# A gated linear-attention layer and a mixture of experts on one core: batches interleaved, decays scanned over 128-token blocks

## Chip, core and metric

The kernel runs on one core of a Trainium2 chip. The metric is the time of one execution in device microseconds (us), the median of the runs. The core has a matrix engine (PE, with its weight loads as PEld), a vector engine (DVE), a scalar engine (ACT), a general engine (POOL), and a sync engine (SP) that in this kernel issues DMAs only. Each engine works through its own list in order and stops at an instruction whose inputs or buffers are not ready.

## The reference

Two layers follow each other. The first is attention with a decaying state, for 4 batches, 8 heads, 768 tokens, head width 48:

```python
for t in range(S):
    state = alpha[:, :, t, :, None] * state + einsum('bhd,bhe->bhde', k[:, :, t], v[:, :, t])
    y[:, :, t] = einsum('bhd,bhde->bhe', q[:, :, t], state)
```

`alpha` lies in 0.8 to 1 and decays each key dimension by itself. The heads of a token are put side by side to x of 4 x 768 x 384. The second layer sends each token to one of 8 experts (384 to 1024 to 384 with a ReLU) and scales the result with that expert's softmax probability. The expert is the argmax of the token's logits at a batch's first token or where `local_gate < 0.5`; elsewhere it is the expert of the token before.

## The kernel before

**Blocks.** The 3072 tokens are worked in 24 blocks of 128 tokens, each of two chunks of 64, in the order of the batches: batch 0's six blocks, then batch 1's, and so on. Two heads share 112 partitions (odd head rows 0 to 47, even head rows 64 to 111), so the 8 heads are four pairs.

**One block** passes these steps (the loop is L462 to L485):

- `load`, `load_v` (L239, L250): SP issues the transfer `x` (keys, queries and decays together), two transfers into `vt` (values for the state, even and odd heads in two halves with zeros beside them) and two into `vw` (the same values again, under room for the states). These have three buffers (NP) and are asked for two blocks ahead.
- `prep` (L257): two DVE scans over 520 columns: `A`, the prefix products of the decays in each 64-token chunk (L264), and `sf`, a backward scan seeded with the reciprocal of the chunk's last product (L267). POOL multiplies keys by `sf` and queries by `A` (L268, L270).
- `kt` (L278): four PE transposes of the keys; ACT copies them out of PSUM as `kk`.
- `um` (L302): 8 matmuls give `up`, the sum of key times value for each chunk. For each chunk DVE adds it to the state (`tt`, L322) and decays the state to the chunk's end (`sn`, L323); ACT copies that state into `vw` (L327, L328). The state of one chunk is needed by the next, all through a batch.
- `pm` (L287): 16 matmuls of keys by queries into `pe`; ACT copies the scaled queries under them (L297, L298); two DVE masks of 64 partitions x 512 columns (L300) make `pq`.
- `ym` (L330): 16 matmuls, each of 112 or 128 rows, take masked products and state part in one go (L338); ACT copies the sum out as `XR` (L344).
- `xt` (L346): three transposes of x, an ACT copy `xx`, the store of x to DRAM (`xd`, L355), and three matmuls for the router's logits (L357).

**Routing** (`route`, L360) runs for every two blocks (G = 2). DVE finds the winning expert, scans along 256 tokens on 8 partitions for the sticky choice (`em`, L389) and for the token's place in its expert's list (L391); POOL scatters probability and token number into the lists (`ls`, L420), one indirect DMA per block.

**Experts.** From block 12 on the first 240 tokens of experts 0 and 1 are worked in pieces between the attention's steps (`early`, L429); each expert's weights come in seven transfers (`rw`, L102 and L111) and are split into two parts by ACT, POOL and DVE. When the attention is through, all the other expert work follows (L492 on).

**Order.** The order on each engine is set at build time by a scheduler that simulates the program; `tc.high_priority()` pulls routing and the early experts ahead. `dense` (L234) puts matmuls of zeros on PE in the first 15 blocks.

## Time and profile before

| what | before |
|---|---|
| median of 3 runs | 528.54 us (524.2, 528.54, 528.86) |
| span of the profiled execution | 522.5 us |
| PE busy in the span | 459.4 us, 88% |
| DVE busy in the span | 309.6 us, 59% |
| ACT busy in the span | 211.3 us, 40% |
| POOL busy in the span | 228.3 us, 44% |
| mean granted TensorE clock | 0.894 |
| moved by DMA | 70.98 MB, 136 GB/s on the mean |

The span is the time from the profiled execution's first instruction to its last, and lies 6.04 us under the median of the runs. "Busy" counts the time in which an engine runs something. A row of a grouped view reads: line, engine, operation, output <- input, shapes, count, then busy us and mean ns of one, then the idle time just before these instructions and what ended it. In the table of windows each row is one stretch of the span, in us from its start.

### The profile page before, as it was taken

What the parts mean: (1) busy time and instruction counts of PE and PEld (TensorE: products, weight loads), DVE (VectorE), ACT (ScalarE), POOL (GpSimd) and SP (SyncE); (2) the same over time, 40 slices, a digit from 0 to 9 for tenths busy, and PEclk for the clock granted to TensorE, in tenths of its full rate; (3) what the DMA queues carried; (4) which work ended last, traced back from release to release, by engine and by line L of the source; (5) the groups of instructions that cost most, each with busy time, mean ns of one, the idle gap of its engine ahead of it and who ended that gap; (6) DMA issues with size and microseconds to landing.
All of it is one profiled execution on the core that took longest, in us unless ns stands there. A gap on an engine that the chain in (4) does not pass through costs nothing. (4 is left out here: it accounts for less than half of the span.)

```text
span 522.5 us, 10340 instructions
## 1 busy us (share of the span) xinstructions
PE 459.4 (88%) x3916; PEld 407.4 (78%) x3916; DVE 309.6 (59%) x626; ACT 211.3 (40%) x444; POOL 228.3 (44%) x205
## 2 busy tenths in 40 slices
PE   6696785799779899689969999999999999999990
PEld 5584674577668787578859989899898998999990
DVE  5779959889977989698423534434334343252420
ACT  2445452645644454575214442433423433233210
POOL 7224445336435633643352565352554443723301
PEclk9679767858885799989979999999999999999996
DMA  8955687743857643975030645525356353450100
GB/s 197 221 147 145 150 265 156 209 102 108 191 152 163 170 102 99 248 216 188 1 86 22 203 127 189 152 81 142 112 156 177 90 159 118 136 176 2 46 3 26
DMA packets 31082, 70.98 MB, mean 136 GB/s; under 512 B 8096, under 2 KB 17579, under 8 KB 31031
## 3 DMA queue, kind: packets, MB, share of 16 engines
q1 hardware_dynamic: 24758, 59.14, 42.1%
q0 software_dynamic: 4864, 10.66, 7.0%
q10 hardware_dynamic: 1409, 0.50, 0.4%
q8 instruction: 32, 0.52, 0.4%
q14 instruction: 19, 0.16, 0.1%
HBM read 60.76 MB, written 10.70 MB: 137 GB/s over the span
## 5 line engine op out<-in xcount | busy, mean ns | idle before, releaser
L168 DVE SCALAR_TENSOR_TENSOR hl<-h,hh 128x480 fp32r<-128x480 f32 (+1 forms) x80 | 44.2, 555 | 81.2 <-ACT hh L167 81.1
L167 ACT ACTIVATE hh<-h 128x480 fp32r<-128x480 f32 (+1 forms) x80 | 39.0, 490 | 82.0 <-PE h L163 82.0
L270 POOL TENSOR_TENSOR x<-x,A 112x512 f32<-112x512 f32 x24 | 29.9, 1245 | 72.2 <-DVE A L264 27.3
L137 POOL DMA_INDIRECT xg<-xd,li x32 | 34.5, 1079 | 47.3 <-DMA li<-ls 32.3
L187 POOL DMA_INDIRECT out<-yo,li x32 | 33.3, 1042 | 49.3 <-DVE yo L186 42.9
L338 PEld LDWEIGHTS y<-vw,pq 112*64 112x64 f32 (+1 forms) x768 | 37.1, 169 | 22.3 <-DVE pq L300 14.3
L338 PE MATMUL y<-vw,pq 112*64 112x48 f32 (+1 forms) x768 | 44.6, 259 | 11.1 <-DVE pq L300 10.3
L186 DVE TENSOR_SCALAR yo<-yp,li 120x384 f32<-120x384 f32 x32 | 19.5, 615 | 47.0 <-PE yp L181 47.0
L268 POOL TENSOR_TENSOR x<-x,sf 112x512 f32<-112x512 f32 x23 | 28.2, 1224 | 31.0 <-DVE sf L267 17.7
L267 DVE TENSOR_TENSOR_SCAN sf<-x,z 112x520 f32<-112x520 f32 x24 | 37.6, 1567 | 0.9
L420 POOL DMA_INDIRECT ls<-pl,ix x24 | 25.4, 1060 | 25.8 <-DVE em L389 7.2
L295 PE MATMUL pe<-x 48*64 48x64 f32 x384 | 35.8, 250 | 0.4 <-POOL x L270 0.4
L296 PE MATMUL pe<-x 48*64 48x64 f32 x384 | 35.9, 249 | 0.0
L264 DVE TENSOR_TENSOR_SCAN A<-x,z 112x520 f32<-112x520 f32 x24 | 29.6, 1235 | 9.5 <-DMA x<-akq 9.2
L300 DVE TENSOR_TENSOR pq<-pe,cs 64x512 f32<-64x512 f32 x48 | 32.9, 685 | 3.5 <-PE pe L296 2.4
L295 PEld LDWEIGHTS pe<-x 48*64 48x64 f32 x384 | 30.4, 159 | 4.6 <-issue 2.5
L296 PEld LDWEIGHTS pe<-x 48*64 48x64 f32 x384 | 30.3, 158 | 1.9 <-issue 1.6
L327 ACT COPY vw<-sn 48x192 f32<-48x192 f32 x44 | 15.3, 348 | 37.1 <-DVE sn L323 30.7
L357 PE MATMUL xp<-wgs,xx 128*128 128x128 f32 x144 | 29.6, 357 | 0.5 <-ACT xx L354 0.5
L311 PE MATMUL up<-vt,kk 128*48 128x96 f32 x192 | 27.9, 294 | 1.1 <-ACT kk L284 1.1
L313 PE MATMUL up<-vt,kk 128*64 128x96 f32 x192 | 28.7, 298 | 0.0
L357 PEld LDWEIGHTS xp<-wgs,xx 128*128 128x128 f32 x144 | 24.8, 250 | 2.8 <-ACT xx L354 0.9
(233 smaller groups left out, 1364.5 us busy)
## 6 DMA issues: line engine op xcount, KB each, us to landing
x<-akq SPq DMA_DIRECT2D x23, 675.9 KB, 6.1
vt<-vn SPq DMA_DIRECT2D x48, 96.0 KB, 4.4
vw<-vw SPq DMA_DIRECT2D x48, 96.0 KB, 2.9
xd<-XR SPq DMA_DIRECT2D x24, 192.0 KB, 4.0
rw_a<-w SPq DMA_DIRECT2D x3, 512.0 KB, 6.0
rw_a<-w SPq DMA_DIRECT2D x4, 384.0 KB, 7.7
rw_1a<-w SPq DMA_DIRECT2D x3, 512.0 KB, 6.0
rw_1a<-w SPq DMA_DIRECT2D x4, 384.0 KB, 9.1
```

The source lines that it names most:

```text
L137: g_.indirect_dma_start(out=xg, out_offset=None, in_=xd[0:self.rows], in_offset=bass.IndirectOffsetOnAxis(ap=self.li.bitcast(I32)[:, s, 2: ...
L167: s_.activation(hh, h, AF.Relu)
L168: v_.scalar_tensor_tensor(hl, h, 0.0, hh.bitcast(F32), ALU.max, ALU.subtract)
L187: apart(outs, g_.indirect_dma_start(out=out, out_offset=bass.IndirectOffsetOnAxis(ap=self.li.bitcast(I32)[:, s, 1:2], axis=0), in_=yo, in_ ...
L264: v_.tensor_tensor_scan(A, a[:, 0:SW], z1, 0.0, ALU.mult, ALU.add)
L267: v_.tensor_tensor_scan(sf[:, ::-1], a[:, SW:0:-1], z2[0:R, ::-1], 0.0, ALU.mult, ALU.add)
L270: g_.tensor_tensor(q2, q2, A3[:, :, 1:], ALU.mult)
L295: t_.matmul(pe[0:64, hp, w], lhsT=k[64:112, hp, w], rhs=q[64:112, hp, w], start=True, stop=True)
L296: t_.matmul(pe[64:128, hp, w], lhsT=k[0:48, hp, w], rhs=q[0:48, hp, w], start=True, stop=True)
L300: v_.tensor_tensor(pq[r, par], pe[r], cc("tri")[r].unsqueeze(1).broadcast_to([64, HP, 128]), ALU.mult)
L338: t_.matmul(yw[c * C:(c + 1) * C, h * D:(h + 1) * D], lhsT=d["pq"][r, par, hp, c * C:(c + 1) * C], rhs=d["vv"][r, par, c, hp * D:(hp + 1) ...
L357: t_.matmul(xp[:, DM:], lhsT=xx[:, k * 128:(k + 1) * 128], rhs=wgs[:, k, :], start=(k == 0), stop=(k == 2))
```

## The change

**Order of the blocks.** Block i is now block i // 4 of batch i % 4, so the four batches' states advance side by side and a state is used again only four blocks later (`st["S", i % G]`). G becomes 4, so one group to be routed holds one block of each batch.

**Decays.** The scans run over a whole block of 128 tokens in place of each chunk. POOL sets the decay slot at the second chunk's start to one (L256), and the scan starts at 2^40 (SEED) instead of 1; the new state is scaled back by 1/SEED. The decays now have a tile `a` of their own (L241, two buffers), and `x` holds keys and queries alone (L243, four buffers).

**Values.** `vw` is gone. One transfer brings a block's values into the lower columns of `vt` by token (L249), and an ACT copy moves the first 64 tokens' values to the other half (L250).

**States.** One DVE add over 384 columns forms both chunk sums (L317), two ACT copies put the states before both chunks into `sb` (two buffers, L319 and L320), and one DVE instruction decays the state for the batch's next block (L323).

**Products.** `pe` lies in two PSUM banks with both heads and both chunks on 128 partitions, so a single DVE mask of 128 x 512 suffices (L294) and the ACT copies of queries are gone. `ym` is 8 matmuls of queries by state (L335) and 16 of masked products by values (L340).

**Routing.** The logits of four blocks are formed at the group's end (12 matmuls, M = 32, L368), then transposed. The sticky scan runs on 32 partitions (four blocks by eight experts) over 128 tokens (L398); the places in the lists come from two matmuls with ones and a triangle (L411, L413) rather than a scan. There are four scatters per group instead of two (24 in all, as before).

**PSUM.** `kp` and `xp` share one buffer named "tr".

The core of the diff:

```diff
+SEED = 2.0 ** 40
...
-G = 2                       # blocks routed together
+G = B
...
-    wgs = cp.tile([128, 3, 128], F32, name="wgs")
+    wgs = cp.tile([128, 3, 32], F32, name="wgs")
...
-        v_.memset(z1[:, 0:SW:C + 1], 1.0)
+        v_.memset(z1[:, 0:SW:2 * (C + 1)], SEED)
...
+            sb = ap.tile([R, 2, 2, CW], F32, bufs=1, name=f"sb{j}")
+            g_.memset(sb[0:64], 0.0)
+            g_.memset(sb[64:112, :, 1, :], 0.0)
+            SBs.append(sb)
...
         def load(i):
-            x = ap.tile([R, 2 * BW + SW + 1], F32, tag="x", bufs=3, name=f"x_{i}")
-            vt = VTs[i % NP]
-            if i == 0:
-                nc.sync.dma_start(x[:, 2 * BW:], akq[:, i, 2 * BW:])
-                nc.sync.dma_start(x[:, 0:2 * BW], akq[:, i, 0:2 * BW])
-            else:
-                nc.sync.dma_start(x, akq[:, i, :])
...
-            blk[i] = dict(x=x, vt=vt, vv=vv, pq=PQs[i % NP])
+            at = i % G * NBB + i // G
+            a = ap.tile([R, SW + 1], F32, tag="a", bufs=2, name=f"a_{i}")
+            nc.sync.dma_start(a, akq[:, at, 2 * BW:])
+            x = ap.tile([R, 2 * BW], F32, tag="x", bufs=4, name=f"x_{i}")
+            nc.sync.dma_start(x, akq[:, at, 0:2 * BW])
+            blk[i] = dict(a=a, x=x, vt=VTs[i % NP], sb=SBs[i % 2])
         def load_v(i):
...
-            for par in range(2):
-                rr = slice(64 * par, 64 * par + 64)
-                nc.sync.dma_start(vt[rr, par], vn[rr, i * DM:(i + 1) * DM])
-                nc.sync.dma_start(vv[rr, par].rearrange("p c d -> p (c d)"), vw[rr, i * DM:(i + 1) * DM])
+            at = i % G * NBB + i // G
...
+            nc.sync.dma_start(vt[:, 1, :], vn[:, at * DM:(at + 1) * DM])
+            s_.copy(vt[0:64, 0, :], vt[0:64, 1, :])
...
+            g_.memset(a[:, C + 1:SW:2 * (C + 1)], 1.0)
             A = ap.tile([R, SW], F32, tag="A", bufs=2, name=f"A_{i}")
             v_.tensor_tensor_scan(A, a[:, 0:SW], z1, 0.0, ALU.mult, ALU.add)
-            v_.reciprocal(z2[0:R, C:SW:C + 1], A[:, C:SW:C + 1])
+            end = slice(2 * C + 1, SW, 2 * (C + 1))
+            v_.reciprocal(z2[0:R, end], A[:, end])
             sf = ap.tile([R, SW], F32, tag="sf", bufs=1, name=f"sf_{i}")
             v_.tensor_tensor_scan(sf[:, ::-1], a[:, SW:0:-1], z2[0:R, ::-1], 0.0, ALU.mult, ALU.add)
...
+            d["end"] = A[:, end]
...
-            if i % NBB == 0:
-                g_.memset(vv[64:112, 0, 0, :], 0.0)
-                g_.memset(vv[0:48, 1, 0, :], 0.0)
...
         def pm(i):
...
-            pe = pp.tile([128, HP, 128], F32, tag="pe", name=f"pe_{i}")
...
+            pe = pp.tile([128, 2, 512], F32, tag="pe", name=f"pe_{i}")
+            for b_ in range(2):
...
-                for c in range(2):
+                for (par, c) in ((0, 0), (1, 1), (0, 1), (1, 0)):
...
-            s_.copy(pq[64:112, 0], q[64:112])
-            s_.copy(pq[0:48, 1], q[0:48])
-            for (r, par) in ((slice(0, 64), 0), (slice(64, 128), 1)):
-                v_.tensor_tensor(pq[r, par], pe[r], cc("tri")[r].unsqueeze(1).broadcast_to([64, HP, 128]), ALU.mult)
+                    r = slice(0, 48) if par else slice(64, 112)
+                    t_.matmul(pe[c * C:(c + 1) * C, par, hp * C:(hp + 1) * C], lhsT=k[r, hp, w], rhs=q[r, hp, w],
...
+            pq = ap.tile([128, 2, HP, C], F32, tag="pq", bufs=2, name=f"pq_{i}")
+            v_.tensor_tensor(pq, pe[:, :, 0:HP * C].rearrange("p e (h t) -> p e h t", h=HP),
+                             cc("tri")[:, 0:C].unsqueeze(1).unsqueeze(1).broadcast_to([128, 2, HP, C]), ALU.mult)
+            d["pq"] = pq
         def um(i):
...
+            kk, vt, sb = st["kk", i], d["vt"], d["sb"]
+            if i < G:
+                s3 = ap.tile([R, 3, HP, D], F32, tag="st", bufs=G + 2, name=f"st_{i}")
+                g_.memset(s3[:, 0], 0.0)
...
                 t_.matmul(uw[0:64, n], lhsT=kk[:, hp, 0:64], rhs=vt[:, :, (2 * hp + 1) * D:(2 * hp + 2) * D],
...
-            for c in range(1 if i % NBB == NBB - 1 else 2):
-                ae = d["A"][:, :, c, C:C + 1].broadcast_to([R, HP, D])
-                sn = ap.tile([R, HP, D], F32, tag="sn", name=f"sn_{i}_{c}")
-                if i % NBB == 0 and c == 0:
-                    v_.tensor_tensor(sn, up[0:R, c], ae, ALU.mult)
...
-                    tt = ap.tile([R, HP, D], F32, tag="tt", name=f"tt_{i}_{c}")
-                    v_.tensor_tensor(tt, up[0:R, c], st["S"], ALU.add)
-                    v_.tensor_tensor(sn, tt, ae, ALU.mult)
-                st["S"] = sn
-                vv, cn = (d["vv"], 1) if c == 0 else (blk[i + 1]["vv"], 0)
-                sf = sn.rearrange("p h d -> p (h d)")
-                s_.copy(vv[64:112, 0, cn, :], sf[64:112])
-                s_.copy(vv[0:48, 1, cn, :], sf[0:48])
+            n = 2 if i + G < NB else 1
+            v_.tensor_tensor(s3[:, 1:1 + n], up[:, 0:n], s3[:, 0].unsqueeze(1).broadcast_to([R, n, HP, D]), ALU.add)
+            sf = s3.rearrange("p c h d -> p c (h d)")
+            s_.copy(sb[64:112, :, 0, :], sf[64:112, 0:2])
+            s_.copy(sb[0:48, :, 1, :], sf[0:48, 0:2])
+            if n == 2:
+                sn = ap.tile([R, 3, HP, D], F32, tag="st", bufs=G + 2, name=f"st_{i + G}")
+                v_.scalar_tensor_tensor(sn[:, 0], s3[:, 2], 1.0 / SEED, d["end"].unsqueeze(2).broadcast_to([R, HP, D]),
+                                        ALU.mult, ALU.mult)
+                st["S", i % G] = sn
         def ym(i):
...
+                for c in range(2):
+                    t_.matmul(yw[c * C:(c + 1) * C, 2 * hp * D:2 * (hp + 1) * D], lhsT=d["q"][:, hp, c * C:(c + 1) * C],
...
             for h in range(H):
-                hp, par = h // 2, h % 2
...
                 for c in range(2):
-                    t_.matmul(yw[c * C:(c + 1) * C, h * D:(h + 1) * D], lhsT=d["pq"][r, par, hp, c * C:(c + 1) * C],
-                              rhs=d["vv"][r, par, c, hp * D:(hp + 1) * D], start=True, stop=True)
+                    r = slice(c * C, (c + 1) * C)
+                    t_.matmul(yw[r, h * D:(h + 1) * D], lhsT=pq[r, h % 2, h // 2, :], rhs=vt[r, h * D:(h + 1) * D],
...
+            s_.copy(d["XR"], yw[:, 0:DM])
...
-            xp = pp.tile([128, 512], F32, tag="xp", name=f"xp_{i}")
...
+            xp = pp.tile([128, DM], F32, tag="tr", name=f"xp_{i}")
...
-            s_.copy(xx, xp[:, 0:DM])
-            nc.sync.dma_start(xd[1 + i * 128:1 + (i + 1) * 128], XR[:, o, :])
...
-                t_.matmul(xp[:, DM:], lhsT=xx[:, k * 128:(k + 1) * 128], rhs=wgs[:, k, :], start=(k == 0), stop=(k == 2))
-            s_.copy(L[:, o, :], xp[:, DM:DM + E + 1])
...
+            s_.copy(xx[:, o].rearrange("p k t -> p (k t)"), xp)
+            nc.sync.dma_start(xd[1 + i * 128:1 + (i + 1) * 128], XR)
...
+            lg = pp.tile([128, 128], F32, tag=RT, name=f"lg_{g}")
+            for k in range(3):
+                for b in range(n):
+                    t_.matmul(lg[32 * b:32 * (b + 1), :], lhsT=wgs[:, k, :], rhs=xx[:, b, k, :], start=(k == 0), stop=(k == 2))
+            lc = rt([128, 128], "lc")
...
+            lt = pp.tile([128, n, 32], F32, tag=RT, name=f"lt_{g}")
...
-            v_.tensor_tensor_scan(em[0:8], km, rp[0:8], 0.0 if first else st["E"], ALU.mult, ALU.add)
...
-            v_.tensor_tensor_scan(em[32:40], em[0:8], z8, cc("base", 0, 8) if g == 0 else st["c"], ALU.add, ALU.add)
...
+            em = rt([8 * n, 128], "em")
+            v_.tensor_tensor_scan(em, km, rp[:, 0, :], st["E"] if g else 0.0, ALU.mult, ALU.add)
...
+            v_.tensor_tensor_scan(oi.rearrange("p e b -> p (e b)"), m5.rearrange("p e b -> p (e b)"), oh.rearrange("p e b -> p (e b)"), 0.0,
+                                  ALU.mult, ALU.add)
+            pw = pp.tile([128, E, n + 1], F32, tag=RT, name=f"pw_{g}")
+            t_.matmul(pw.rearrange("p e b -> p (e b)"), lhsT=one, rhs=oi.rearrange("p e b -> p (e b)"),
+                      start=True, stop=False)
+            t_.matmul(pw[:, :, 0:n], lhsT=trif, rhs=o4, start=False, stop=True)
+            ps = rt([128, E, n + 1], "ps")
...
+        g_.memset(one, 1.0)
+        g_.memset(m5, 1.0)
+        g_.memset(m5[:, :, 0], 0.0)
+        for e in range(E):
+            g_.memset(c0[:, e:e + 1], float(e * RS - 1))
+            g_.memset(c1[:, e:e + 1], float(e * RS - 1 + (C1 if e in EARLY else 0)))
+        g_.tensor_copy(trif, cc("tri"))
```

What this does to the order, in three places. ACT, before, around the end of block 10: `XR` is the block's output, `vw` receives the states, `pq` the scaled queries, `xx` the transposed x, `oh` belongs to the routing. The brackets name what an instruction waits for.

```order
L344 COPY XR_1221<-y_1298 128x384 [waits PE_49]
L327 COPY vw_95<-sn_0_1347 48x192 [waits DVE_49]
L328 COPY vw_95<-sn_0_1347 48x192
L297 COPY pq_100<-x_1224 48x512 [waits DMAHW5_49,Pool_49]
L298 COPY pq_100<-x_1224 48x512
L354 COPY xx_1384<-xp_1380 128x384 [waits PE_49,Activation_49]
L399 COPY oh_1178<-rb_1173 128x16 [waits PE_49]
L327 COPY vw_102<-sn_1_1353 48x192 [waits DVE_49]
L328 COPY vw_102<-sn_1_1353 48x192
L344 COPY XR_1456<-y_1438 128x384 [waits DMAHW3_49,PE_49]
```

The same engine in the changed kernel: `XR_1264` is the output of block 9, `vt_91` gets the values of block 12, `sb_97` the states of block 10, `XR_1353` is the output of block 10, `vt_93` is for block 13 and `sb_102` for block 11.

```order
L346 COPY XR_1264<-y_1238 128x384 [waits DMAHW7_49,PE_49]
L250 COPY vt_91<-vt_91 64x384 [waits DMAHW5_49]
L319 COPY sb_97<-st_866 48x2x192 [waits DVE_49,Activation_49]
L320 COPY sb_97<-st_866 48x2x192 [waits Activation_49]
L355 COPY xx_1174<-xp_1321 128x384 [waits PE_49]
L346 COPY XR_1353<-y_1327 128x384 [waits DMAHW6_49,PE_49]
L277 COPY kk_1374<-kp_1369 128x448 [waits PE_49,Activation_49]
L250 COPY vt_93<-vt_93 64x384 [waits DMAHW1_49]
L319 COPY sb_102<-st_955 48x2x192 [waits DVE_49,Activation_49]
L320 COPY sb_102<-st_955 48x2x192 [waits Activation_49]
```

Between two outputs there were four copies of states and two of queries; now there are a copy of values that waits for a transfer, and two copies of states right behind it. The copy of values is that of the block two ahead of the states beside it.

SP in the changed kernel, two blocks' worth of transfers, up to the one that the `vt` copy at the head of these rows needs (`vt_91`) and the store behind it:

```order
L241 DMA a_1266<-akq 112x521 [waits DMAHW7_49,DVE_49]
L243 DMA x_1268<-akq 112x1024 [waits PE_49]
L249 DMA vt_95<-vn 128x384 [waits DMAHW1_49,PE_49]
L356 DMA xd<-XR_1175 128x384 [waits DMAHW2_49,Activation_49]
L241 DMA a_1355<-akq 112x521 [waits DMAHW3_49,DVE_49]
L243 DMA x_1357<-akq 112x1024 [waits DMAHW4_49,PE_49]
L249 DMA vt_91<-vn 128x384 [waits DMAHW5_49,PE_49]
L356 DMA xd<-XR_1264 128x384 [waits DMAHW6_49,Activation_49]
```

Each block now has four transfers there (`a`, `x`, `vt`, `xd`) where it had six. The transfer into `vt` waits for PE, which has last read that buffer in `ym` three blocks before.

DVE in the changed kernel, from one block's state add to the next one's:

```order
L317 TENSOR_TENSOR st_866<-up_1287,st_866 112x384
L323 SCALAR_TENSOR_TENSOR st_1300<-st_866,A_1184 112x192
L258 SCALAR_TENSOR_TENSOR A_1362<-a_1266,z_84 112x520
L260 RECIPROCAL z_85<-A_1362 112x4
L262 SCALAR_TENSOR_TENSOR sf_1365<-a_1266,z_85 112x520
L294 TENSOR_TENSOR pq_1319<-pe_1302,cs 128x512
L294 TENSOR_TENSOR pq_1408<-pe_1391,cs 128x512
L317 TENSOR_TENSOR st_955<-up_1376,st_955 112x384
```

Four state instructions a block have become two, two masks one; the scans and the reciprocal stand as they did.

152 lines of the change are left out of this document (77 added, 75 removed).

## The prediction

> **What bounds the kernel now.** I read the table of windows first, with the span cut where the kernel changes its work: start, attention (two halves), the passage to the experts, the experts, the end.
>
> ```profile
> core 0: us, PE busy (x) PEld busy (x) DVE busy (x) ACT busy (x) POOL busy (x), PEclk, DMA share, GB/s
> 0.00:23.00 23.00, 16.02 (x157) 12.81 (x157) 14.20 (x21) 7.35 (x14) 12.66 (x30) 0.78 0.89 206
> 23.00:134.00 111.00, 89.65 (x1108) 73.40 (x1108) 96.65 (x200) 55.60 (x137) 47.94 (x45) 0.77 0.62 162
> 134.00:245.00 111.00, 95.07 (x1199) 79.86 (x1196) 95.44 (x222) 59.86 (x144) 52.72 (x46) 0.85 0.66 171
> 245.00:270.00 25.00, 19.99 (x133) 17.12 (x131) 9.46 (x39) 4.80 (x15) 10.84 (x11) 0.96 0.15 44
> 270.00:500.00 230.00, 229.39 (x1273) 215.32 (x1272) 91.26 (x143) 82.60 (x134) 102.11 (x72) 0.99 0.41 121
> ```
>
> From 270 to 500 us PE is busy 229.39 of 230 us at a granted clock of 0.99: the experts are bound by PE, and the change takes nothing out of that stretch. All it can move lies ahead of 270 us. From 23 to 245 us DVE is busy 96.65 + 95.44 = 192.1 of 222 us, more than any other engine; PE's 184.7 us are at a clock of 0.77 and 0.85, so part of that is slow running. The block outputs give the pace, in the view of one source line:
>
> ```profile
> L344 ACT COPY XR<-y x24: 467/479/481, 23.0 to 244.4; 128x384 f32<-128x384 f32 x24
> ```
>
> 24 outputs from 23.0 to 244.4 us are 23 intervals of 221.4 / 23 = 9.63 us a block. What DVE does there, grouped by line and shape (count, then busy us and mean ns, then idle before):
>
> ```profile
> L267 DVE TENSOR_TENSOR_SCAN sf<-x,z 112x520 f32<-112x520 f32 x22 | 34.3, 1558 | 0.9
> L300 DVE TENSOR_TENSOR pq<-pe,cs 64x512 f32<-64x512 f32 x44 | 30.2, 686 | 3.5 <-PE pe L296 2.4
> L264 DVE TENSOR_TENSOR_SCAN A<-x,z 112x520 f32<-112x520 f32 x21 | 25.9, 1235 | 2.1 <-DMA x<-akq 1.8
> L323 DVE TENSOR_TENSOR sn<-tt,A 112x192 f32<-112x192 f32 x39 | 24.7, 633 | 0.9
> L322 DVE TENSOR_TENSOR tt<-up,sn 112x192 f32<-112x192 f32 x39 | 13.7, 352 | 11.0 <-PE up L313 10.4
> L391 DVE TENSOR_TENSOR_SCAN em<-em,c,z 8x256 f32<-8x256 f32 x10 | 9.5, 954 | 0.3
> L265 DVE RECIPROCAL z<-A 112x8 f32<-112x8 f32 x21 | 4.1, 197 | 0.3
> ```
>
> The idle before these rows is small except before `tt` (11.0 us, for PE's `up`): DVE is the bound, and the chunk-to-chunk chain adds to it. Per block scans, masks and states cost 1.56 + 2 x 0.69 + 1.24 + 2 x 0.63 + 2 x 0.35 + 0.20 = 6.3 us.
>
> **What the change takes off DVE.** One mask of 0.69 goes: 128 partitions x 512 columns hold as many columns as 64 x 512, and I take the same 0.69 (bounds 0.69 and twice that, which would be no gain). One `sn` of 0.63 goes. Two `tt` of 0.35 become one add of twice the columns, 0.55 to 0.70; I take 0.55. The list scan of 0.95 per two blocks goes, 0.48 a block. DVE is busy 192.1 / 23 = 8.35 us a block, routing and early experts included; less 0.69, 0.63, 0.15 and 0.48 that is a floor of 6.4 us a block. If DVE stayed the bound, 9.63 - 6.4 = 3.2 us a block would be gained.
>
> **What the change adds: a loop through a DMA.** I do not believe that floor is reached, because of the order on ACT and SP shown above. On ACT the copy `vt` (L250) for block i+3 stands ahead of the copies `sb` (L319, L320) for block i+1. Behind the waiting copy are `sb`, `xx`, `XR` and `kk`; PE's `ym` of block i+1 waits for `sb`. The copy waits for a transfer that waits for PE: `vt` has three buffers, and the last reader of that buffer is `ym` of block i. So: end of `ym`(i), transfer of `vt`(i+3), copy `vt`, copies `sb`(i+1), `ym`(i+1). In the kernel before, the same wait for a free buffer exists on SP, but no engine's list stood behind it. For the transfer I use the view of DMA issues (count, size of each, us from issue to landing):
>
> ```profile
> x<-akq SPq DMA_DIRECT2D x23, 675.9 KB, 6.1
> vt<-vn SPq DMA_DIRECT2D x48, 96.0 KB, 4.4
> vw<-vw SPq DMA_DIRECT2D x48, 96.0 KB, 2.9
> xd<-XR SPq DMA_DIRECT2D x24, 192.0 KB, 4.0
> rw_1a<-w SPq DMA_DIRECT2D x3, 512.0 KB, 6.0
> rw_1a<-w SPq DMA_DIRECT2D x4, 384.0 KB, 9.1
> ```
>
> The new `vt` has 192 KB on 128 partitions, as `xd` has: 4.0 us. Its bounds are 2.9 (half the bytes, `vw`) and 6.1 (`x`, since an `x` load of 459 KB now stands just ahead of it on SP and may share the engines).
>
> *A rule beside this row.* The Trainium skill, page "SBUF — State Buffer", section "The DMA setup-cost knee (why "@ 1 MiB" ≠ asymptote)", gives a transfer about 2 us plus its bytes at 436 GB/s, which would be an estimate of 2.45 us for 192 KB. The trace does not agree for the same size: `xd` took 4.0. By the rule this loop would end near 6.4 us a block, and the time at the first rival's 480 us.
>
> The copies, from ACT's groups in the same window (count, busy us, mean ns):
>
> ```profile
> L328 ACT COPY vw<-sn 48x192 f32<-48x192 f32 x42 | 14.8, 352 | 0.8
> L298 ACT COPY pq<-x 48x512 f32<-48x512 f32 x22 | 13.6, 618 | 0.3
> ```
>
> 192 columns take 0.352 and 512 take 0.618 us, a slope of 0.83 ns a column; each of the three new copies has 384 columns, 0.51 us, 1.53 together (1.2 if they went like `XR` at 0.479 with overlaps; 1.9 at the 512-column row).
>
> For `ym` I need the pace of small matmuls, from the timeline of PE (start, duration) in a fast and in a slow stretch:
>
> ```profile
> 43.88 0.25 PE L311 MATMUL up<-vt,kk 128*48 128x96 f32 x1
> 43.96 0.25 PE L311 MATMUL up<-vt,kk 128*48 128x96 f32 x1
> ...
> 48.49 0.22 PE L296 MATMUL pe<-x 48*64 48x64 f32 x1
> 48.55 0.22 PE L296 MATMUL pe<-x 48*64 48x64 f32 x1
> ...
> 53.43 0.37 PE L311 MATMUL up<-vt,kk 128*48 128x96 f32 x1
> 53.59 0.37 PE L311 MATMUL up<-vt,kk 128*48 128x96 f32 x1
> ```
>
> ```profile
> L338 PE MATMUL y<-vw,pq 112*64 112x48 f32 (+1 forms) x768 | 44.6, 259 | 11.1 <-DVE pq L300 10.3
> ```
>
> The last row, from the page, counts 768 matmuls for 24 x 16 calls: each call runs as two. A pair (the two heads' halves side by side) of 96 columns starts every 0.08 us in the fast stretch and every 0.16 us in the slow one; the pairs of 64 columns in `pe` come every 0.06 us. The new `ym` has 8 calls of 96 columns, so 16 matmuls in 8 pairs of the two chunks, and 16 calls of 48 columns, 16 pairs: 8 x 0.08 + 16 x 0.06 = 1.6, and 0.25 for the last to end, 1.85 us. I take 2.2 us, at the granted clock of 0.85 (1.85 / 0.85). Bounds: 1.85 at the full clock, and 3.4 at half (1.6 x 2 + 0.25).
>
> *A second rule.* The Trainium skill, page "TensorE: Matmul & The Clock Gate", section "What's actually happening", says that the clock is halved by default and is full only after about 3.4 us of steady work, and falls back after an idle window as long. The trace agrees with two speeds, 0.08 and 0.16 us for the same pair, and the loop leaves PE idle during each transfer; by the rule alone `ym` would take 3.4 us and the loop 9.2, the fourth rival. The dense matmuls of the first 15 blocks are kept, and the windows' mean of 0.77 to 0.85 speaks for a mix.
>
> So one turn of the loop is 0.1 (hop to SP and on) + 4.0 + 0.05 + 1.53 + 0.1 (to PE) + 2.2 = 8.0 us. PE's own work then lies beside the wait: its share of a block is (89.65 + 95.07) / 23 = 8.0 us at a reduced clock, about 6.5 at the full one; the change adds 8 pairs of 0.08, 0.64 us, to `ym`, and logits on a quarter of the columns may give as much back. The loop, PE and DVE (6.4) are then close together, and the loop decides. To be sure of its length I add 8 us over the whole: the seven weight transfers for each of the two early experts pass through SP between the blocks', and land in 6.0 to 9.1 us instead of 4.0; I take 4 us for each expert (bounds 0 and 10 for each).
>
> **Start.** Block 0's scan now follows POOL's memset of the slot in `a` (L256), which the order puts behind the memsets of all constants, 32 POOL instructions.
>
> ```profile
> 4.93 1.24 DVE L264 TENSOR_TENSOR_SCAN A<-x,z 112x520 f32<-112x520 f32 x1 [2.54 <-DMA x<-akq]
> ...
> 1.67 0.42 POOL L214 MEMSET vt<- 64x384 f32 x1
> ...
> 0.26 0.12 POOL L669 MEMSET const-float32-1.0<- 128x1 f32 x1
> ```
>
> Three of 0.42, two of twice that and two of about half, and some 20 small ones of up to 0.12, from 0.7 us on, with gaps between: I put the scan at about 7 us, so 2 us late (bounds 0 and 4).
>
> **The passage to the experts.** The last group now routes four blocks, not two, so two more scatters lie on the way to the last list. From POOL's timeline:
>
> ```profile
> 256.89 0.97 POOL L420 DMA_INDIRECT ls<-pl,ix  x1 [3.70 <-DVE pl L417]
> 258.16 0.97 POOL L420 DMA_INDIRECT ls<-pl,ix  x1 [0.30 <-issue]
> ```
>
> They start 1.27 us apart: 2.5 us. Logits for four blocks at the group's end instead of along the way add about 1 us, fewer DVE scans take off about 0.5. Sum 3 us (bounds 0 and 6).
>
> **Sum.** Attention: 23 x 8.0 + 8 = 192.0 against 221.4, -29.4. Start +2, passage +3, experts 0. 522.5 - 24.4 = 498.1 us of span; the median lay 528.54 - 522.5 = 6.04 us above that profile's span, so 504.1, said as 504 us. Its own range: a loop of 7.1 (landing 3.4, `ym` 1.85) to 8.9 us (4.9, the rest as taken) gives 483 to 525.
>
> **Rivals.**
>
> First, the wait is hidden and DVE becomes the bound. Transfers issued early land at 2.9 us, `ym` runs at 1.85: the loop is 0.25 + 2.9 + 1.53 + 1.85 = 6.5, level with DVE's 6.4; with small waits I take 6.9. Then 23 x 6.9 + 8 = 166.7, -54.7, and +5: 479 us, said as 480. For it: `vw` did land at 2.9, and a block moves 1076 KB in place of the 1252 KB of the DMA rows (676 + 4 x 96 + 192). Against it: the `x` load just ahead.
>
> Second, PE decides in the second half. There PE is busy 95.07 of 111 us with the early experts' matmuls between, and needs most of them still. The first half takes 11.5 x 8.0 + 8 = 100 instead of 111 us, the second 111 as before; less 11, and +5 for start and passage: 522.5, rounded with half of the bound on the passage to 525 us, no change. Against it: clock 0.85 there, so part of the 95 us is slow running that shorter waits mend.
>
> Third, slower: the `vt` transfer lands as late as the `x` transfer did, 6.1 us, since it follows one in the same queue. The loop is then 8.0 + 2.1 = 10.1 us, 23 x 10.1 + 8 = 240.3, +18.9, and +5 +6.04: 552 us. It decides from a period of 9.1 us on (9.63 less (8 + 5) / 23), a landing of 5.1 us. For it: `vt` itself took 4.4 us at half the bytes.
>
> Fourth, the loop's idle keeps PE at its slow pace: `ym` takes 3.4 us (pairs at 0.16 and 0.12), the loop 8.0 + 1.2 = 9.2, 23 x 9.2 + 8 = 219.6, -1.8, +5 +6.04: 532 us, no change. For it: the slow pairs above; against it: the clock was 0.77 to 0.85 on the mean with waits between, and other matmuls fill the gap.
>
> That the change does not do what it says would be a scheduler that puts the `vt` copies behind the `sb` copies; the order shows that from block 19 on and for two early ones, so it is part of the range.
>
> **How the numbers follow.** Forecast 0.55 (504 us), first rival 0.18 (480), second 0.08 (525), third 0.14 (552), fourth 0.05 (532). A measurement of this kernel can tell about 1% from no change, 523.3 to 533.8 us. Forecast and first rival are faster: 0.73; the second and fourth are the same: 0.13; the third slower: 0.14. The range of 8 in 10 goes down to 474 (the first rival without its losses at start and passage) and up to 536 (a loop of 9.3 us: 23 x 9.3 + 8 = 221.9, +0.5 +5 +6.04), leaving out most of the third.
>
> **What would show it.** Right: the block outputs' line stands about 8 us apart; the waits of ACT's L250 for the DMA into `vt`, and of PE's L335 for the `sb` copies, are among the longest; DVE's busy share in the attention falls below 0.85; that DMA's row reads near 4 us; the experts' stretch keeps its 230 us at 0.99. Wrong: no idle before L250 and DVE at nine tenths (first rival), PE at nine tenths in the second half only (second), a `vt` row of 5 us or more (third); and a span of the expert stretch other than 230 us would break the ground of the sum.

## The result and the profile after

The changed kernel takes 560.28 us (median of 4 runs, 555.22 to 565.95) against 528.52 us before: 1.0607 times as long, with an interval of 1.0521 to 1.0692. On a second chip it was 565.7 us, 1.0759 (1.0696 to 1.0822). The forecast was 504 us. The profile below is the one from the second chip (559.54 us, span 557.4 us), because the profiled run of the first was a disturbed one: a run more than 1.5% above the fastest of its kernel counts as disturbed, the ratios leave such runs out, and none is given where a single run is left.

The table of windows first, cut at the first output, the twelfth, the last, and at the experts' stretch:

```profile
core 0: us, PE busy (x) PEld busy (x) DVE busy (x) ACT busy (x) POOL busy (x), PEclk, DMA share, GB/s
...
25.20:134.20 109.00, 82.46 (x1206) 60.99 (x1207) 70.73 (x106) 38.20 (x81) 43.57 (x49) 0.77 0.50 138
134.20:274.20 140.00, 115.52 (x1495) 91.36 (x1496) 75.81 (x144) 50.70 (x113) 56.40 (x58) 0.84 0.43 129
274.20:311.00 36.80, 19.18 (x124) 16.90 (x125) 7.75 (x31) 5.08 (x15) 12.49 (x12) 0.72 0.16 44
311.00:541.00 230.00, 230.00 (x1289) 216.49 (x1288) 89.73 (x142) 82.29 (x134) 97.88 (x68) 1.00 0.39 117
```

The same cut of the kernel before, at its own first, twelfth and last output:

```profile
23.00:128.90 105.90, 85.56 (x1053) 70.09 (x1053) 91.71 (x188) 52.85 (x130) 45.59 (x41) 0.76 0.63 164
128.90:244.40 115.50, 98.57 (x1244) 82.57 (x1241) 99.82 (x233) 62.13 (x150) 55.07 (x49) 0.85 0.65 169
```

And the outputs' line:

```profile
L346 ACT COPY XR<-y x24: 463/480/483, 25.2 to 274.2; 128x384 f32<-128x384 f32 x24
```

The experts' stretch is as it was, PE busy all through at a granted clock of 1.00. The first output comes 2.2 us later, the time from first to last output is 249.0 us in place of 221.4 (+27.6), and what follows the last output takes 283.2 in place of 278.1 us (+5.1): together the 34.9 us by which the span grew. The second half loses most: 140.0 us for twelve blocks, 11.7 each, where it was 9.6. DVE did become lighter: busy 146.5 us of 249.0 in the attention, where it was 191.5 of 221.4. Its groups (count, busy us and mean ns, idle before), in the window from 25 to 274 us:

```profile
L262 DVE TENSOR_TENSOR_SCAN sf<-a,z 112x520 f32<-112x520 f32 x21 | 38.3, 1825 | 1.6
L258 DVE TENSOR_TENSOR_SCAN A<-a,z 112x520 f32<-112x520 f32 x21 | 26.9, 1281 | 1.2
L294 DVE TENSOR_TENSOR pq<-pe,cs 128x512 f32<-128x512 f32 x22 | 14.9, 676 | 23.2 <-PE pe L291 23.2
...
L317 DVE TENSOR_TENSOR st<-up,st 112x384 f32<-112x384 f32 x18 | 9.9, 552 | 13.4 <-PE up L314 13.0
L323 DVE SCALAR_TENSOR_TENSOR st<-st,A 112x192 f32<-112x192 f32 x18 | 7.9, 438 | 0.7
```

One mask of 0.68 us for two, one add of 0.55 for two of 0.35, one decay where there were two: as priced. The mask now waits 23.2 us for PE, where it waited 2.4; the add waits 13.0 us, where `tt` waited 10.4 already. The longest wait in the attention is a new one on ACT (the view of waits gives the total in us, how often, and the longest):

```profile
ACT vt L250 <- DMA vt<-vn: 54.7, 18, 10.7
```

One turn of it, from the output of block 9 to that of block 10. ACT's timeline (start, duration, line, then the idle before and what ended it):

```profile
113.10 0.48 ACT L346 COPY XR<-y 128x384 f32<-128x384 f32 x1 [1.24 <-PE y L340]
118.26 0.51 ACT L250 COPY vt<-vt 64x384 f32<-64x384 f32 x1 [4.68 <-DMA vt<-vn]
118.80 0.51 ACT L319 COPY sb<-st 48x384 f32<-48x384 f32 x1
119.33 0.51 ACT L320 COPY sb<-st 48x384 f32<-48x384 f32 x1
...
124.10 0.48 ACT L346 COPY XR<-y 128x384 f32<-128x384 f32 x1 [3.88 <-PE y L340]
```

SP's and PE's in the same stretch:

```profile
113.21 0.38 SPq L249 DMA_DIRECT2D vt<-vn  x1
...
124.09 0.35 SPq L249 DMA_DIRECT2D vt<-vn  x1
```

```profile
109.88 0.88 PE L335 MATMUL y<-sb,x 112*64 112x96 f32 x16 [1.65 <-ACT sb L320]
...
119.89 1.55 PE L335 MATMUL y<-sb,x 112*64 112x96 f32 x16 [3.84 <-ACT sb L320]
```

`ym` ends at 113.1, SP issues the transfer at 113.21, ACT starts the copy when it has landed at 118.26, the states follow, PE begins the next `ym` at 119.89 and ends it at 124.1, where SP issues the next transfer. That is the loop of the prediction, closed. The two rows of PE also show two speeds: the same 16 matmuls take 0.88 us or 1.55 us.

### The profile page after: what moved, and what is told of

Its sections match the earlier page's. It is cut to its first block, busy times and chain, and to the rows that moved or that the text cites. A ratio compares the mean times of both kernels' runs of the same rounds, so it can differ in the third digit from the quotient of the medians.

```text
span 563.9 us, 10709 instructions
## 1 busy us (share of the span) xinstructions
PE 484.8 (86%) x4301; PEld 414.8 (74%) x4301; DVE 259.8 (46%) x446; ACT 183.0 (32%) x350; POOL 226.6 (40%) x239
## 5 line engine op out<-in xcount | busy, mean ns | idle before, releaser
L262 DVE TENSOR_TENSOR_SCAN sf<-a,z 112x520 f32<-112x520 f32 x24 | 44.2, 1843 | 1.8
L340 PEld LDWEIGHTS y<-vt,pq 64*64 64x64 f32 x768 | 33.5, 164 | 8.0 <-issue 5.2
L340 PE MATMUL y<-vt,pq 64*64 64x48 f32 x768 | 38.9, 251 | 0.5 <-issue 0.5
L335 PE MATMUL y<-sb,x 112*64 112x96 f32 x384 | 29.8, 307 | 6.9 <-ACT sb L320 6.9
L291 PEld LDWEIGHTS pe<-x 48*64 48x64 f32 x768 | 22.8, 170 | 17.1 <-issue 9.1
L291 PE MATMUL pe<-x 48*64 48x64 f32 x768 | 31.5, 273 | 4.1 <-POOL x L265 4.1
L258 DVE TENSOR_TENSOR_SCAN A<-a,z 112x520 f32<-112x520 f32 x24 | 30.6, 1277 | 7.7 <-POOL a L256 6.3
L335 PEld LDWEIGHTS y<-sb,x 112*64 112x64 f32 x384 | 23.1, 175 | 14.0 <-ACT sb L320 10.1
L312 PEld LDWEIGHTS up<-vt,kk 128*48 128x48 f32 x192 | 21.9, 157 | 14.2 <-ACT kk L277 10.9
L294 DVE TENSOR_TENSOR pq<-pe,cs 128x512 f32<-128x512 f32 x24 | 16.3, 678 | 29.5 <-PE pe L291 29.5
## 6 DMA issues: line engine op xcount, KB each, us to landing
x<-akq SPq DMA_DIRECT2D x24, 448.0 KB
a<-akq SPq DMA_DIRECT2D x24, 227.9 KB
```

The lines of the kernel that those rows point to most:

```text
L262: v_.tensor_tensor_scan(sf[:, ::-1], a[:, SW:0:-1], z2[0:R, ::-1], 0.0, ALU.mult, ALU.add)
L291: t_.matmul(pe[c * C:(c + 1) * C, par, hp * C:(hp + 1) * C], lhsT=k[r, hp, w], rhs=q[r, hp, w], start=True, stop=True)
L312: t_.matmul(uw[64:112, n], lhsT=kk[:, hp, 64:112], rhs=vt[:, :, 2 * hp * D:(2 * hp + 1) * D], start=True, stop=True)
L335: t_.matmul(yw[c * C:(c + 1) * C, 2 * hp * D:2 * (hp + 1) * D], lhsT=d["q"][:, hp, c * C:(c + 1) * C], rhs=sb[:, c, :, hp, :], start=(hp = ...
L340: t_.matmul(yw[r, h * D:(h + 1) * D], lhsT=pq[r, h % 2, h // 2, :], rhs=vt[r, h * D:(h + 1) * D], start=False, stop=(h == H - 1), skip_gro ...
```

## The experiments

Two theories were put against each other at first. The **loop theory**: ACT's waiting copy ties each `ym` to the one before through a DMA, and the loss is this loop. The **PE rival**: PE, at a low clock and with more to do, is the bound, and ACT's wait lies beside it. Ratios are to the kernel before on the same chip, where its median lay between 524.22 and 528.13 us.

### The changed kernel once more, and four buffers

```diff
-NP = 3
+NP = 4
```

> The changed kernel itself once more, for a second profile beside the others. Both theories: about 560 us (555 to 566), some 6% above the kernel before, block outputs about 11 us apart.

> Four buffers for vt instead of three, nothing else. The order on ACT now puts the vt copy of block i+4 ahead of the sb copies of block i+1, so the loop ym(i), transfer, vt copy, sb copies, ym(i+1) is closed just as before. Loop theory: no gain, 553 to 567 us, and L250 still waits 40 us or more for the transfer. Rival (there are simply too few buffers, so the transfer starts late): the transfer starts a block earlier, 4 us a block are hidden, 530 us or less. Rival (PE at its low clock is the bound and ACT's wait lies beside it): no change either.

The changed kernel again: 565.7 us, 1.0759. With four buffers: 560.22 us, 1.0655 (1.0596 to 1.0715). L250's wait stays:

```profile
ACT vt L250 <- DMA vt<-vn: 49.9, 18, 6.7
```

More buffers don't open the loop, since the copy for a block one further ahead stands at the same place before the states. The rival of too few buffers falls. The PE rival expected no change here either, so this run doesn't decide between it and the loop.

### The copy replaced, and the copy pinned

In the first kernel a second transfer of 96 KB fills the other half of `vt`:

```diff
-            s_.copy(vt[0:64, 0, :], vt[0:64, 1, :])
+            nc.sync.dma_start(vt[0:64, 0, :], vn[0:64, at * DM:(at + 1) * DM])
```

> The values' second half comes by a second transfer of 96 KB on SP in place of the ACT copy; three buffers as in the changed kernel, and the transfers still wait for ym of three blocks before. ACT no longer waits for a transfer. Loop theory: the turn of 4.1 (transfer) + 0.5 (copy) is out of the path from block output to block output, 23 times some 2 to 3 us after PE's own work fills in: 505 to 535 us. PE rival (PE busy 217 of 256 us at a clock of 0.73): 553 to 567 us. It also costs DMA time, 96 KB a block.

In the second the copy stays and is pinned on ACT behind the state copies of the block before:

```diff
-            s_.copy(vt[0:64, 0, :], vt[0:64, 1, :])
+            if i == 0:
+                s_.copy(vt[0:64, 0, :], vt[0:64, 1, :])
...
             s_.copy(sb[0:48, :, 1, :], sf[0:48, 0:2])
+            if i + 1 < NB:
+                nv = blk[i + 1]["vt"]
+                tc.keep_in_program_order(s_.copy(nv[0:64, 0, :], nv[0:64, 1, :]))
```

> The same work as the changed kernel, instruction for instruction; only the ACT copy into vt for block i+1 is pinned behind the sb copies of block i, so it waits for ym of block i-2, which is long done. Loop theory: as the run with two loads without its extra transfer, 500 to 535 us, and L250 waits under 10 us in all. PE rival: 553 to 567 us, with the idle before L250 gone but PE as busy as now.

Two loads: 552.67 us, 1.0437 (1.0351 to 1.0524), above the 505 to 535 that the loop theory gave, and just under the 553 where the rival began. Pinned: 537.58 us, 1.0172 (1.0092 to 1.0253), just above the 500 to 535. The same instructions in another order are 28 us faster than the changed kernel on the same chip, where the PE rival expected no gain. (The scheduler moved other instructions along with the pinned one; the 28 us are the price of the order as a whole.) The copy's line in the pinned kernel has no wait entry left, so nothing stands under the two headings:

```profile
L324 ACT COPY vt<-vt x23: 506/507/509, 20.1 to 243.2; 64x384 f32<-64x384 f32 x23
its engine sat idle before it (us, times) until:
who waited for it (us, times):
```

So the loop is real and costs most of the difference to before (0.0587 of 0.0759 in the ratio). But with it gone the kernel is still no faster than before, although its DVE has less to do: the loop was not the whole of the error.

### The attention by itself

Three kernels have the early experts moved to the end of the attention: the kernel before, the changed one and the pinned one. All work is still done. All three have the same edits (`HL` lists the PSUM buffers that the early experts may use when the attention is through):

```diff
-HL = ("h", "kp", "pe")
+HL = ("h", "pe")
...
-            if i == T1 - LW:
+            if i == NB - LW:
...
-            if i == T1:
+            if i == NB - 1:
```

> The kernel before, with the early experts' weights and pieces moved from blocks 6 and 12 to the end of the attention (blocks 18 and 23); nothing is left out. It shows the attention by itself. Both theories: block outputs 8.5 to 9.3 us apart (its first six stand 8.8 apart), 195 to 215 us from the first to the last; the total is longer than 527 us, since the experts no longer fill gaps.

> The changed kernel with the same move of the early experts. Loop theory: the loop is closed in every block, so outputs stand 7.5 to 9 us apart (its first six stand 7.6), with 30 us or more of waiting at the vt copy. Rival (PE at a low clock is the bound of the attention itself): 9.5 us or more, no better than the kernel before with the same move.

> The kernel with the pinned vt copy, with the same move of the early experts. Loop theory: 6.5 to 7.5 us between outputs from first to last, 150 to 172 us, the DVE floor that the prediction worked out; then what keeps the pinned kernel from beating the kernel before is the second half, where the early experts share PE. Rival: within 5% of the run without the pin.

Totals: 553.73 us, 1.0513 (1.0443 to 1.0584) for the kernel before; 557.51 us, 1.0585 (1.0507 to 1.0663) for the changed one; 531.21 us, 1.0031 (0.9977 to 1.0085) for the pinned one. The line of the outputs in each, in that order:

```profile
L344 ACT COPY XR<-y x24: 461/479/481, 22.1 to 229.5; 128x384 f32<-128x384 f32 x24
```

```profile
L346 ACT COPY XR<-y x24: 462/478/480, 24.4 to 252.7; 128x384 f32<-128x384 f32 x24
```

```profile
L350 ACT COPY XR<-y x24: 472/478/482, 22.2 to 227.0; 128x384 f32<-128x384 f32 x24
```

From first to last that is 9.0, 9.9 and 8.9 us a block. From block 18 on the early experts' weights come in; up to block 17 (172.1, 180.1 and 152.0 us in ACT's timelines) it is 8.8, 9.2 and 7.6 us. So the change without the loop is worth 1.2 us a block where PE has only the attention, and the loop costs 1.5, more than all of it. The sizes expected of the loop theory for the changed and the pinned kernel (up to 9, and 6.5 to 7.5) were too small. Both results also lie where the PE rival put them: the changed kernel at 9.5 us or more and no better than the kernel before, the pinned one within 5% of the changed one (4.7% less). By their totals these two runs don't decide; the outputs' line does, 204.8 us with the pin against 228.3 without.

The second finding is in the totals. Moving the early experts to the end costs the kernel before 25 us: there they filled time in which PE otherwise waits. In the pinned kernel it costs nothing (1.0031 against 1.0172). With the move, the pinned kernel is 22.5 us faster than the kernel before with the same move (531.21 against 553.73), near the 24 us of the forecast, 20 of them up to block 17: where PE isn't shared, the change pays once the loop is out.

### What is left in the pinned kernel

Seven further edits, each on the pinned kernel, tried the things that its profile shows beside PE. More matmuls of zeros, for the clock:

```diff
-DN, TF = (0, 1, 1, 0), T1 + 3
+DN, TF = (0, 1, 1, 0), NB
```

> The pinned kernel, with the matmuls of zeros kept on through all 24 blocks instead of 15 (two more matmuls in each of nine blocks, 0.22 to 0.43 us each). If a low granted clock in the second half is what is left of the loss: a higher clock from 190 us on and 3 to 15 us less than the pinned kernel's 538. If PE's time is short there whatever its clock: 4 to 8 us more.

```diff
-DN, TF = (0, 1, 1, 0), T1 + 3
+DN, TF = (0, 2, 2, 0), NB
```

> The pinned kernel with four matmuls of zeros in every block instead of two in the first fifteen: 66 more of them, 0.22 us each at the full clock, 0.43 at half. Clock theory (the smaller matmuls of the change leave PE at its slow clock even when it has no wait): granted clock up by 0.03 or more in the attention, and 520 to 534 us. If PE's time alone counts: 15 to 28 us more, above 550.

537.93 us with the few (no ratio; the runs go from 525.2 to 540.85 us, so this one is undecided) and 542.85 us, 1.0363 (1.029 to 1.0437), with the many. With the many the granted clock from block 11 to 23 was 0.92 and the blocks there came 11.0 us apart; in the four pinned kernels below that have a ratio the clock was 0.76 to 0.89 and the blocks came 10.3 to 11.4 us apart. So the clock was higher and the total did not fall: above the 520 to 534 us of the clock theory. The 15 to 28 us that 66 zero matmuls would cost by time alone did not show either (5 us by the medians).

The decays' transfer and POOL's memset behind it, which POOL waits for 38 us:

```diff
-            g_.memset(a[:, C + 1:SW:2 * (C + 1)], 1.0)
...
-            a = ap.tile([R, SW + 1], F32, tag="a", bufs=2, name=f"a_{i}")
+            a = ap.tile([R, SW + 1], F32, tag="a", bufs=4, name=f"a_{i}")
...
     ap[..., 1:] = _pairs(alpha, 1.0)
+    ap[:, :, :, 1, 0] = 1.0
```

> The pinned kernel, with the ones at the second chunk's slot laid in the input beside the decays instead of POOL's memset (L256), and four buffers for the decays instead of two. POOL's 38 us of waiting for the decays' transfer go. If that wait is what is left of the loss (a second loop: sf, transfer of decays, memset, A): 515 to 528 us. If PE and the clock are what is left: 534 to 541 us, as the pinned kernel.

542.64 us, 1.0338 (1.0226 to 1.045): no gain, so that wait lay beside the bound. The same with the early experts from block 16 on:

```diff
-HL = ("h", "kp", "pe")
+HL = ("h", "pe")
...
-T1 = 12
+T1 = 16
```

> As the run before, and the early experts start after block 16 instead of 12 (their weights from block 10 on), with two buffers fewer for their last hidden tiles. If the early experts' share of PE is what eats the gain in the second half: 518 to 530 us, between the pinned kernel (538) and the same with the experts at the end (531) or below both. If their place does not matter: 534 to 541 us.

539.29 us, without a ratio: the four runs go from 529.54 to 542.18 us, and whether this helps is undecided. The routing without its raised priority:

```diff
-                    with tc.high_priority():
-                        route((i - 1) // G)
+                    route((i - 1) // G)
```

> The pinned kernel, with the routing of four blocks at its own place in the program's order instead of ahead of it. In the profile of the pinned kernel every fourth interval is 4 to 8 us longer than the others (a chain over PE, ACT and DVE, then four scatters on POOL). If the raised priority makes that lump: 525 to 534 us. If the chain costs the same wherever it stands: 534 to 541; and it can get worse, 545 or more, if the early experts then start late.

540.88 us, 1.031 (1.0268 to 1.0353): no gain, rather a loss, since the pinned kernel's interval ends at 1.0253. The early experts' weights on POOL's queue, and a fifth buffer for them:

```diff
-            tc.keep_in_program_order(nc.sync.dma_start(o, i))
+            tc.keep_in_program_order(g_.dma_start(o, i))
```

> The pinned kernel, with the early experts' weights issued on POOL's queue instead of SP's, so that no block's transfer stands behind them on SP. If the weight transfers ahead of the blocks' own make the 10 us a block from block 5 to 11 (7.9 where the weights come late): 8 to 9 us there and 520 to 532 us. If it is the splitting of the weights on ACT, POOL and DVE, or PE: 534 to 545 us.

```diff
-RW = 4
+RW = 5
```

> The pinned kernel with five buffers for weights as loaded instead of four, so that the fifth transfer of an expert does not stand on SP until the first is split. If SP's wait for those buffers (5.8 us in all in the pinned kernel's profile) holds up the blocks: 525 to 533 us. If not: 534 to 545 us.

546.9 us, 1.0414 (1.0321 to 1.0507), worse, and 530.16 us, 1.0142 (1.0067 to 1.0217), which the pinned kernel's own interval includes. In the last one the outputs run from 24.3 to 240.5 us, 216.2 us and so 5 us less than before; start and passage give 10.6 back: 1.3 at the start, and 287.4 us after the last output instead of 278.1.

### PE's extra work, put into the kernel before

The kernel before, with nothing changed but that `ym` is preceded by eight calls on zeros, of the shape of the new `q` by state products. They write columns that `ym` then overwrites, so the result is the same:

```diff
+            for hp in range(HP):
+                for c in range(2):
+                    t_.matmul(yw[c * C:(c + 1) * C, 2 * hp * D:2 * (hp + 1) * D], lhsT=dz.bitcast(F32)[0:R, 0:C],
+                              rhs=dz.bitcast(F32)[0:R, 64:64 + 2 * D], start=True, stop=True)
             for h in range(H):
```

> The kernel before, with eight calls of 64 x 96 columns of zeros ahead of ym's own in each block: the extra PE work that the change puts into ym (16 matmuls, 0.64 us a block at the full clock), alone. If PE has room in the kernel before (DVE is the bound): within 1% of 527 us. If PE is the bound in the second half already: 8 us more or beyond, 535 to 545 us, and that is what is left of the pinned kernel's loss.

547.79 us, 1.0437 (1.0355 to 1.0519). The windows of its profile, cut at the twelfth and the last output:

```profile
22.00:126.00 104.00, 85.43 (x1201) 69.79 (x1203) 92.87 (x185) 51.52 (x127) 45.15 (x41) 0.87 0.62 168
126.00:266.40 140.40, 123.10 (x1507) 101.31 (x1505) 107.89 (x245) 65.09 (x158) 60.70 (x53) 0.84 0.53 142
```

The first half takes 104.0 us (105.9 without the zeros): there PE's extra work costs no time. PE is busy as long as before (85.4 us, 85.6 without the zeros), at a granted clock of 0.87 instead of 0.76; why the clock is higher is open. The second half takes 140.4 us (115.5): there it costs 25 us, 2.1 a block, at a clock of 0.84 (0.85). The 16 matmuls of a block themselves last 0.88 us at the fast pace and 1.55 at the slow one in this trace. PE's rows in the second half, two of this run and the last of the kernel before:

```profile
L336 PE MATMUL y<-dz 112*64 112x96 f32 x192 | 14.6, 293 | 0.0
...
L163 PE MATMUL h<-xh,w1h_1a 128*128 128x240 f32 x13 | 4.6, 356 | 0.0
```

```profile
L163 PE MATMUL h<-xh,w1h_1a 128*128 128x240 f32 x3 | 0.9, 308 | 0.0
```

The zeros account for 14.6 us, 1.2 a block. The rest goes with another shift: counted over all its rows, 46 of the 240 matmuls of expert 1's early part run before the last output, where it was 11. What follows the last output gets no shorter by that (279.4 us, 278.1 without the zeros), since PE is idle for 12.9 us of the 60 after it instead of 5.6. So in the second half, with the early experts among the blocks, PE had little time to spare in the kernel before already; and the change adds this work to every block.

### All that helped, together

The pinned kernel with the early experts at the end, five weight buffers and the ones laid in the input (the diffs above):

> What the runs so far point to, put together: the pinned vt copy, the early experts at the end of the attention (where PE is not shared with them until block 18), five buffers for weights as loaded, and the ones laid in the input. If PE's shared second half was what was left of the loss and the three edits add up: 517 to 526 us, up to 1.5% under the kernel before on the same chip. If they do not add up: 527 to 534 us, no gain over the kernel before.

537.55 us, 1.0144 (1.0066 to 1.0221), above both ranges. The edits don't add up; no version was found that is faster than the kernel before.

## Why the prediction was wrong

**What bounds before: half right.** DVE bounds the first half, as far as the run with zeros shows: PE's extra work costs nothing there. For the second half I took the same from DVE's busy share, 95.4 of 111 us, with PE's 95.1 beside it. That was wrong: more work on PE made that half longer. And of the 3.2 us a block that would be gained "if DVE stayed the bound", the pinned kernel with five weight buffers gained 1.2 in the first half (92.9 us instead of 105.9) and lost 0.65 in the second (123.3 instead of 115.5).

**DVE's relief: right.** The durations came as priced (0.68, 0.55), and the attention by itself went from 8.8 to 7.6 us a block once the loop was out. The floor of 6.4 was never reached over more than a few blocks; the first five intervals of the pinned kernel with late experts have a mean of 6.8 us (5.6 to 8.2), at a granted clock of 1.00.

**The loop: found, and mis-sized.** Its place, its order and its links are those of the trace. By its terms, taken block by block from the timelines of ACT, SP and PE in the profile of the second chip:

| term of one turn | predicted | measured |
|---|---|---|
| transfer, issue to copy | 4.0 us | 4.2 us (mean of 21; 2.4 to 7.0) |
| three copies | 1.53 us | 1.53 us |
| `ym`, first matmul to output | 2.2 us | 3.6 us (mean of 24; 1.99 to 6.5) |
| hops | 0.25 us | as taken |
| one turn | 8.0 us | 9.6 us |

The transfer was right, by the row of `xd`. By the Trainium skill, page "SBUF — State Buffer", section "The DMA setup-cost knee (why "@ 1 MiB" ≠ asymptote)", 192 KB would land in an estimated 2.45 us; the trace gives 4.2, and only its fastest landings come near (2.40 and 2.48).

**`ym` is the step that failed first.** Undisturbed it takes 1.99 us, close to the 1.85 worked out. But other matmuls stand between its calls: the logits, which the change moved to the group's end, in 11 of 24 blocks (18 of them at a time in two), the routing's own matmuls in seven, pieces of the early experts in four. PE also runs part of the calls at its slow pace (1.55 us for the first 16), and in five blocks the output copy starts 0.9 to 3.9 us after PE is done, because ACT is at other work: PE's own part of the mean is 3.1 us. 23 turns of 9.6 are 221 us, 37 more than predicted.

**The lumps: 28 us, not 8.** 249.0 less 221 leaves 28 us, where the prediction added 8 over the whole. They lie in 17.8 and 15.9 us at blocks 7 and 8, where the first expert's weights come in, and in 22.8 and 15.9 at blocks 15 and 16, where its work begins. The transfers of weights through SP, of which the prediction made this term, are not what the trace shows in the longest two. At block 7 a single DVE instruction, which splits a weight, stands ahead of the add of states and lasts 9.58 us beside POOL's split of the others (0.91 to 0.95 us in the kernel before). At block 15 SP's read of the expert's list (L140) waits for the scatters, ahead of the blocks' own transfers, and PE waits for the gathered tokens. The rows of DVE and POOL, then SP's wait and PE's row:

```profile
73.22 9.58 DVE L121 TENSOR_TENSOR w2l_a<-rw_a,w2h_a 128x768 fp32r<-128x768 f32 x1 [4.17 <-ACT w2h_a L120]
```

```profile
75.03 6.94 POOL L112 TENSOR_TENSOR w1l_a<-rw_a,w1h_a 128x1024 fp32r<-128x1024 f32 x3
```

```profile
SPq L140 <- DMA ls<-pl,ix: 10.6, 1, 10.6
```

```profile
176.52 0.86 PE L155 MATMUL tp<-cs,xg 120*128 120x120 f32 x3 [8.87 <-DMA xg<-xd,li]
```

37 and 20 are the 57 us between the predicted -29.4 and the measured +27.6 of the attention.

**Start and passage: nearly right in size.** The first scan starts at 7.86 instead of 4.93 us, 2.9 late, and the first output 2.2 late (2 predicted). The passage cost 5.1 us more (3 predicted). PE is idle for 17.6 of the 60 us after the last output, where it was 5.6: 58 of the 240 matmuls of expert 1's early part now run before that output, where it was 11, and fill this wait no longer. The last group's four scatters are in POOL's timeline, 1.3 us apart:

```profile
289.18 1.01 POOL L441 DMA_INDIRECT ls<-pl,ix  x1 [0.30 <-issue]
290.50 0.99 POOL L441 DMA_INDIRECT ls<-pl,ix  x1 [0.30 <-issue]
291.80 0.98 POOL L441 DMA_INDIRECT ls<-pl,ix  x1 [0.30 <-issue]
293.09 0.98 POOL L441 DMA_INDIRECT ls<-pl,ix  x1 [0.30 <-issue]
```

**The sentence that carried the error** is "PE's own work then lies beside the wait": I set 0.64 us of added pairs against a saving on logits that "may give as much back", and never asked who waits for PE. The run with zeros prices those pairs at 4.4% in the kernel before, the shift of expert 1's work included. The rivals held both halves of it apart. The second ("PE decides in the second half") named the place, but let that half stay at 111 us as if the added work were nothing. The fourth (`ym` at 3.4 us) named the size, and stopped at no change. The third came nearest in time (552 us), with a late transfer that did not happen: luck.

**Sums that don't come out.** The upper end of the range is 534 us by its own terms (522.5 + 0.5 + 5 + 6.04), not 536; the loop of 7.1 us is 7.03; and a block's transfers come to 1060 KB in the units of the DMA rows (227.9 + 448.0 + 192 + 192), not 1076. None of these moves the forecast.

**Settled and open.** Shown: the loop (28 us by the order that pins one copy), 1.2 us a block from the rest of the change in the attention alone, and that PE's extra calls cost the kernel before 23 us, in its second half. What is left of the loss in the pinned kernel is not settled. With five weight buffers its attention is 5 us shorter than that of the kernel before; what it still loses lies in the second half (10.3 us a block, where it was 9.6, with PE busy 108.7 of 123.3 us) and, with 9.3 us, after the last output. That the extra calls account for the first part fits, but was not tried by taking them out: the new layout of `ym` needs them. Each build's order also changes, and no run holds that fixed.

## What to carry to other kernels

When an engine that sets the pace is relieved, ask in each stage which engine is next and how full it is; PE at 85% busy with a granted clock of 0.85 had little room left. A copy that waits for a transfer belongs behind everything on its engine's list that the next block needs; more buffers don't help when the order puts the copy ahead all the same. Where a change adds calls to a second engine, adding just those calls, on zeros, to the kernel before shows in one run where they are free and where not; count what other work moves across the border of the stage with them.

## What the runs showed of the hardware

A scan on DVE takes longer while POOL works on tensors. In the pinned kernel with late experts, the same scan `sf` once beside POOL's multiply and once beside POOL's scatters. DVE's rows, then POOL's:

```profile
55.51 2.02 DVE L263 TENSOR_TENSOR_SCAN sf<-a,z 112x520 f32<-112x520 f32 x1
...
65.25 1.24 DVE L263 TENSOR_TENSOR_SCAN sf<-a,z 112x520 f32<-112x520 f32 x1
```

```profile
55.24 1.18 POOL L267 TENSOR_TENSOR x<-x,A 112x512 f32<-112x512 f32 x1
...
64.92 0.97 POOL L445 DMA_INDIRECT ls<-pl,ix  x1 [0.30 <-issue]
66.19 1.08 POOL L445 DMA_INDIRECT ls<-pl,ix  x1 [0.30 <-issue]
```

0.91 us of POOL's multiply overlap with the first, and it takes 0.78 us longer than the second. The one scan of this run that stands beside 8.2 us of POOL's tensor work lasts 9.67 us. In the changed kernel POOL's work stands beside `sf` more often (17 of its 24 scans take 1.65 us or more, 9 of 24 before); this is why `sf` has a mean of 1.83 us in the changed kernel and 1.56 before, which the prediction did not reckon with. The Trainium skill, page "SBUF — State Buffer", section "Who interferes with whom", says that these two engines share a port pair that one holds exclusively; the trace agrees, 0.78 of 0.91 us.

PE can be busy and slow for long. In the run with two loads, the window from its sixth to its twelfth output:

```profile
63.05:125.33 62.28, 56.98 (x639) 41.75 (x640) 44.72 (x66) 20.26 (x44) 33.23 (x33) 0.61 0.57 144
```

PE is busy 57.0 of 62.3 us at a granted clock of 0.61. Since the ends of matmuls are modelled, short gaps may hide in that busy time.
